# A Fourier mix and a gated block with W_out multiplied by seven products for eight: a second level of the scheme for two of the seven sums, and one PSUM bank per step

## The chip, the cores and the metric

The kernel runs on one core of one Trainium2 chip. The metric is the device time of one execution in microseconds; the time before is the median of three runs. TensorE (PE) multiplies matrices out of SBUF into PSUM[...]. VectorE (DVE) and ScalarE (ACT) can read PSUM; GpSimd (POOL) works on SBUF; SyncE (SP) issues transfers. Each engine works through its own list of instructions in order, and semaphores tie the lists together.

## What is computed

```python
X = np.fft.fft(x, axis=1)          # x: 8 x 3008 x 256, fp32
X = np.fft.fft(X, axis=2)
x = X.real.reshape(24064, 256)
h = x @ w_in                       # 256 x 2048
g = h * (1 / (1 + np.exp(-1.702 * h)))
out = g @ w_out                    # 2048 x 256
```

The transform over the sequence is done first. That over the 256 features is folded into `w_in`. A row k and its mirror row S - k share their cosine part P and their sine part Q: the hidden values are P + Q for one and P - Q (with a term for the Nyquist column, called nb below) for the other. So each step makes P and Q for 256 rows and gets 512 rows of hidden values from them: a forward half and a backward half, which VectorE stores in reversed order.

The products with `w_out` follow the Strassen-Winograd scheme: for a pair of hidden blocks f and the two halves of the rows, the eight 128 x 128 x 256 products become seven, with sums of hidden values (s1 to s4) and of weights (t1 to t4, made once). The seven sums m1 to m7 are kept over eight steps, one group, and added together at the group's end.

## The kernel before: the parts that matter

The loop has 8 x 3 x 2 x 8 = 384 steps (batch, block, half, pair p of hidden blocks). Eight steps make a group. The output products of step t run in loop step t + LAG, LAG = 3. PSUM has four rotating banks (pa, pb, and the transform's) and one bank for each of o0 to o3.

```python
psm = ctx.enter_context(tc.tile_pool(name="psm", bufs=4, space=PS))
pso = ctx.enter_context(tc.tile_pool(name="pso", bufs=1, space=PS))
# [cut]
def halves(out, lhs, rhs, **how):
    for c0 in (0, 64):
        nc.tensor.matmul(out[c0:c0 + 64], lhsT=lhs[:, c0:c0 + 64], rhs=rhs, **how)

def hidden(t):                                     # P into pa, Q into pb
    # [cut]
    for ps, cs in ((pa, 0), (pb, 1)):
        for i in range(2):
            f = 2 * p + i
            halves(ps[:, i * 256:i * 256 + n], wcs[cs][:, f * 128:(f + 1) * 128], pq[:, cs, ks], start=True, stop=True)
    v = sp.tile([128, 512], F32, tag="v", name="v")
    nc.scalar.copy(two(v[:], n), two(pa[:], n))
    vb[t] = v, pa, pb

def rows(t):                                       # forward P + Q, dif = nb * af2 - Q, backward P + dif, reversed
    # [cut]
    nc.vector.tensor_tensor(two(h[:], n), two(v[:], n), two(pb[:], n), op=ALU.add)
    for i in range(2):
        f = 2 * p + i
        nc.vector.scalar_tensor_tensor(dif[:, i * 256:i * 256 + n], nb[:, ks], af2[:, f:f + 1],
                                       pb[:, i * 256:i * 256 + n], op0=ALU.mult, op1=ALU.subtract)
    # [cut: one reversed tensor_tensor of pa and dif into h[:, 1]]

def activate(t):
    # [cut]
    nc.scalar.activation(g, g, ACTF.Gelu_apprx_sigmoid)        # all 1024 columns in one

def sums(t, eng):                                  # s1, s3 on GpSimd; s2, s4 on VectorE
    # [cut]

def product(t):
    # [cut]
    s = st.pop(t)
    plan = ((0, 0, wo[:, p, 0, :], h[:, 0, 0, :n], 0), (0, 1, wt[:, p, 1, :], s[:, 1, :n], 0),
            (1, 0, wo[:, p, 2, :], h[:, 0, 1, :n], 0), (1, 1, wt[:, p, 2, :], s[:, 2, :n], 0),
            (2, 0, wt[:, p, 0, :], s[:, 0, :n], 0), (2, 1, wo[:, p, 3, :], s[:, 3, :n], 0),
            (3, 0, wt[:, p, 3, :], h[:, 1, 1, :n], 0))
    # [cut]
    for q, i, lhs, rhs, f in plan:
        halves(pot[q][:, i, :n], lhs, rhs, start=(p == 0 and i == 0 and f == 0), stop=(p == NP - 1), skip_group_check=True)
    # [cut: at p == NP - 1 ScalarE copies the first sum out of bank o0]

def combine(t):                                    # at the group's end: seven additions and two transposes
    # [cut]
    for out_, i0, i1, how in ((u2, c1, m6, ALU.add), (c11, c1, m2, ALU.add), (u3, u2, m7, ALU.add),
                              (u2, u2, m5, ALU.add), (c12, u2, m3, ALU.add), (c22, u3, m5, ALU.add),
                              (c21, u3, m4, ALU.subtract)):
        nc.vector.tensor_tensor(out_, i0, i1, op=how)
    # [cut]

for t in range(n + LAG):
    if t < n:
        hidden(t)
    # [cut]
    if t >= LAG:
        product(t - LAG)
    # [cut]
    if 0 < t <= n:
        activate(t - 1)
        sums(t - 1, nc.gpsimd)
    sums(t - 2, nc.vector)
    if t < n:
        rows(t)
    if t >= LAG:
        combine(t - LAG)
    for fn, args in extra.get(t, ()):              # transform of the next block or batch: fold1, mix1, stage2, ...
        fn(*args)
```

Of the kernel before, what the change touches and what calls it, by code (L numbers as in the profile page):

```python
# [27 lines left out]
F32 = mybir.dt.float32  # L28
# [15 lines left out]
LAG = 3  # L44
# [67 lines left out]
def kernel(ctx: ExitStack, tc, x, w_in, w_out, tab1, tab2, out):  # L112
# [13 lines left out]
    sp = ctx.enter_context(tc.tile_pool(name="sp", bufs=2, space=SB))  # L126
    op = ctx.enter_context(tc.tile_pool(name="op", bufs=2, space=SB))
    cv = ctx.enter_context(tc.tile_pool(name="cv", bufs=1, space=SB))
    psm = ctx.enter_context(tc.tile_pool(name="psm", bufs=4, space=PS))
    pso = ctx.enter_context(tc.tile_pool(name="pso", bufs=1, space=PS))  # L130
    ctx.enter_context(tc.manual_schedule())

    Xr = [nc.dram_tensor(f"Xr{b}", (NA, NJ, D), F32, kind="Internal").ap() for b in range(B)]
# [16 lines left out]

        return w[rows, jj * NM:jj * NM + 64]

    def bank(name):
        return psm.tile([128, 512], F32, tag="mm", name=name)

# [275 lines left out]
    def differences(n):  # L433
        ps = slice(2 * n, 2 * n + 2)
        b11, b12, b21, b22 = (wo[:, ps, q, :] for q in range(4))
        t1, t2, t3, t4 = (wt[:, ps, q, :] for q in range(4))
        for out, i0, i1 in ((t1, b12, b11), (t2, b22, t1), (t3, b22, b12), (t4, t2, b21)):
            nc.gpsimd.tensor_tensor(out, i0, i1, op=ALU.subtract)

    def fold_w(n):  # L440
# [16 lines left out]

    NP = NF // 2
    steps = [(b, blk, hh, p) for b in range(B) for blk in range(NBLK) for hh in range(2) for p in range(NP)]
    vb, ht, st, pot, ot = {}, {}, {}, {}, {}  # L460

    def width(blk, hh):

        return 225 if (blk, hh) == (0, 1) else 256

    def two(ap, n):
        return free(ap, 0, [256, 2], [1, n])

    def halves(out, lhs, rhs, **how):
        for c0 in (0, 64):  # L470
            nc.tensor.matmul(out[c0:c0 + 64], lhsT=lhs[:, c0:c0 + 64], rhs=rhs, **how)  # L471

    def hidden(t):

        b, blk, hh, p = steps[t]
        n = width(blk, hh)
        pq, ks = pqt[b, blk], slice(hh * 256, hh * 256 + n)
        pa, pb = bank("pa"), bank("pb")
        for ps, cs in ((pa, 0), (pb, 1)):
            for i in range(2):  # L480
                f = 2 * p + i
                halves(ps[:, i * 256:i * 256 + n], wcs[cs][:, f * 128:(f + 1) * 128], pq[:, cs, ks], start=True, stop=True)
        v = sp.tile([128, 512], F32, tag="v", name="v")

        nc.scalar.copy(two(v[:], n), two(pa[:], n))  # L485
        vb[t] = v, pa, pb

    def rows(t):
        b, blk, hh, p = steps[t]
        n = width(blk, hh)  # L490
        nb, ks = nbt[b, blk], slice(hh * 256, hh * 256 + n)
        v, pa, pb = vb.pop(t)
        h = ht[t] = hp.tile([128, 2, 2, 256], F32, tag="h", name="h")
        dif = sp.tile([128, 512], F32, tag="dif", name="dif")
        nc.vector.tensor_tensor(two(h[:], n), two(v[:], n), two(pb[:], n), op=ALU.add)  # L495
        for i in range(2):
            f = 2 * p + i
            nc.vector.scalar_tensor_tensor(dif[:, i * 256:i * 256 + n], nb[:, ks], af2[:, f:f + 1],  # L498
                                           pb[:, i * 256:i * 256 + n], op0=ALU.mult, op1=ALU.subtract)

        full, rest = divmod(n, RUN)
        for at, blocks, m in ((0, full, RUN), (full * RUN, 1, rest)):
            if m:
                ins = [free(x[:], at, [256, 2], [RUN, blocks], [1, m]) for x in (pa, dif)]
                nc.vector.tensor_tensor(free(h[:], 512 + at + m - 1, [256, 2], [RUN, blocks], [-1, m]), *ins, op=ALU.add)  # L505

    def activate(t):
        b, blk, hh, p = steps[t]
        g = free(ht[t][:], 0, [256, 4], [1, width(blk, hh)])
        nc.scalar.activation(g, g, ACTF.Gelu_apprx_sigmoid)  # L510

    def sums(t, eng):

        if not NP <= t < len(steps):
            return
        h, n = ht[t], width(*steps[t][1:3])
        a11, a12, a21, a22 = h[:, 0, 0, :n], h[:, 0, 1, :n], h[:, 1, 0, :n], h[:, 1, 1, :n]
        if eng is nc.gpsimd:
            st[t] = sp.tile([128, 4, 256], F32, tag="s", bufs=3, name="s")
        s1, s2, s3, s4 = (st[t][:, q, :n] for q in range(4))  # L520
        if eng is nc.gpsimd:
            eng.tensor_tensor(s1, a21, a22, op=ALU.add)  # L522
# [2 lines left out]
            eng.tensor_tensor(s2, s1, a11, op=ALU.subtract)  # L525
            eng.tensor_tensor(s4, a12, s2, op=ALU.subtract)  # L526

    def product(t):

        b, blk, hh, p = steps[t]  # L530
        n = width(blk, hh)
        if p == 0:
            for q in range(4):
                pot[q] = pso.tile([128, 2, 256], F32, tag=f"o{q}", name=f"po{q}")
        h = ht.pop(t)
        if t < NP:

            plan = [(half, dh, wo[:, p, 2 * f + dh, :], h[:, half, f, :n], f)
                    for half in range(2) for dh in range(2) for f in range(2)]
        else:  # L540
            s = st.pop(t)
            plan = ((0, 0, wo[:, p, 0, :], h[:, 0, 0, :n], 0), (0, 1, wt[:, p, 1, :], s[:, 1, :n], 0),
                    (1, 0, wo[:, p, 2, :], h[:, 0, 1, :n], 0), (1, 1, wt[:, p, 2, :], s[:, 2, :n], 0),
                    (2, 0, wt[:, p, 0, :], s[:, 0, :n], 0), (2, 1, wo[:, p, 3, :], s[:, 3, :n], 0),
                    (3, 0, wt[:, p, 3, :], h[:, 1, 1, :n], 0))

        if t == len(steps) - 2:
            pot["plan"] = plan
            return
        if t == len(steps) - 1:  # L550
            plan = [it for two_ in zip(pot.pop("plan"), plan) for it in two_]

        for q, i, lhs, rhs, f in plan:
            halves(pot[q][:, i, :n], lhs, rhs, start=(p == 0 and i == 0 and f == 0), stop=(p == NP - 1), skip_group_check=True)
        if p < NP - 1 or t < NP:
            return
        c1 = pot["c"] = op.tile([128, 256], F32, tag="u0", bufs=1, name="u0")
        nc.scalar.copy(c1[:, :n], pot[0][:, 0, :n])  # L558

    def combine(t):  # L560

        b, blk, hh, p = steps[t]
        if p < NP - 1:
            return
        n = width(blk, hh)
        o = op.tile([128, 4, 256], F32, tag="os", name="os")

        def turned(half, src):

            nc.vector.transpose(free(o[:], half * 512, [32, 2], [64, 8], [1, 32]), free(src, 0, [256, 2], [32, 8], [1, 32]))  # L570
            store(b, blk, hh, o, half)

        if t < NP:
            for half in range(2):
                turned(half, pot[half][:])
            return
        c = cv.tile([128, 4, 256], F32, tag="m", bufs=2, name="c")
        if n < 256:
            nc.gpsimd.memset(c[:, :, n:], 0.0)
        (_, m6), (m2, m7), (m5, m3), (m4, _) = ((pot[q][:, 0, :n], pot[q][:, 1, :n]) for q in range(4))  # L580
        u2, u3 = (op.tile([128, 256], F32, tag=f"u{q}", bufs=1, name=f"u{q}")[:, :n] for q in (1, 2))
        c1 = pot["c"][:, :n]
        c11, c12, c21, c22 = (c[:, q, :n] for q in range(4))
        for out_, i0, i1, how in ((u2, c1, m6, ALU.add), (c11, c1, m2, ALU.add), (u3, u2, m7, ALU.add),
                                  (u2, u2, m5, ALU.add), (c12, u2, m3, ALU.add), (c22, u3, m5, ALU.add),
                                  (c21, u3, m4, ALU.subtract)):
            nc.vector.tensor_tensor(out_, i0, i1, op=how)  # L587
            if t == len(steps) - 1:
                if out_ is c12:
                    turned(0, c[:])  # L590
                elif out_ is c22 or out_ is c21:
                    i = int(out_ is c22)
                    nc.vector.transpose(free(o[:], 512 + 32 * i, [64, 8], [1, 32]), free(c[:], (2 + i) * 256, [32, 8], [1, 32]))
        if t == len(steps) - 1:
            store(b, blk, hh, o, 1)
            return
        for half in range(2):
            turned(half, c[:, 2 * half:])

    def store(b, blk, hh, o, half):  # L600

# [136 lines left out]
    at(4, rotate, 0, 4, NG)  # L738
    for i in range(NCK):
        at(7 + i, differences, i)  # L740
    for b in range(B):
        t0 = b * NBLK * NF
        late = 0 if b else 3
# [12 lines left out]
        for blk in range(NBLK):  # L756
            nxt = (b, blk + 1) if blk + 1 < NBLK else (b + 1, 0)
            if nxt[0] < B:
                at(t0 + blk * NF + 8, stage2, *nxt)
                at(t0 + blk * NF + 12, nyquist, *nxt)  # L760

    for t in range(n + LAG):
        if t < n:
            hidden(t)
        if t == 0:
            low_up(in2)
            nyquist(0, 0)
            low_down(in2)
        if t in rows_at:
            first_row(rows_at[t])  # L770
        if t >= LAG:
            product(t - LAG)
        if t in early:
            fold_w(early[t])

        if 0 < t <= n:
            activate(t - 1)
            sums(t - 1, nc.gpsimd)
        sums(t - 2, nc.vector)
        if t < n:  # L780
            rows(t)
        if t >= LAG:
            combine(t - LAG)
        for fn, args in extra.get(t, ()):
            fn(*args)

# [27 lines left out]
```

## Time and profile before

| | before |
|---|---|
| time, median of 3 runs | 1921.33 us (1920.55 to 1921.42) |
| span of the profiled execution | 1919.2 us, granted TensorE clock 0.998 |
| VectorE | 1409.3 us (73%), 2937 instructions |
| GpSimd | 768.2 us (40%), 1057 instructions |
| ScalarE | 674.7 us (35%), 932 instructions |
| output products, 256 columns (L471, tile po) | 8992 records of 379 ns |
| weight loads of 64 columns | 137 ns each |
| gelu of 1024 columns (L510) | 320 of 1060 ns |
| sums on GpSimd, 256 columns (L522, L523) | 624 of 733 and 750 ns |
| sums on VectorE, 256 columns (L525, L526) | 624 of 456 and 487 ns |

The page of the profile gives busy times per engine, a picture of the span in 40 slices, the chain of work that ended last, and the costliest groups of instructions by line, engine and shape. Records of TensorE overlap: a record lasts longer than the time from one to the next, so prices of products are read from starts, not from lengths. An fp32 product appears as two records, and each product is issued in two halves of 64 weight columns. A group's row ends with the idle time of its engine just ahead of it and the instruction that ended that wait.

### The profile page before, as it was taken

Reading aid. Unit: us, or ns where it says so; the run is one execution under the profiler, and the core shown is the slowest. Engines: PE = TensorE matmul, PEld = TensorE weight load, DVE = VectorE, ACT = ScalarE, POOL = GpSimd, SP = SyncE. Lnnn points to the kernel's source line nnn. Section 1 sums busy time; section 2 is a strip of 40 time slices with the busy share of each in tenths; the row PEclk is TensorE's granted clock in tenths of the full one; section 3 lists DMA queues with packets and bytes.
Section 4 is the critical chain, followed back from the end, with each engine's and each line's share of the span. In section 5 each row is a group of like instructions: output and inputs, shape, how many; then the busy total and the mean of one; then the engine's idle time right before and its main releaser. Section 6 shows DMA issues by size and latency. Waiting matters only on the chain.

```text
span 1919.2 us, 46708 instructions
## 1 busy us (share of the span) xinstructions
PE 1907.5 (99%) x19184; PEld 1284.4 (67%) x19184; DVE 1409.3 (73%) x2937; ACT 674.7 (35%) x932; POOL 768.2 (40%) x1057
## 2 busy tenths in 40 slices
PE   9999999999999999999999999999999999999998
PEld 6676666766666666666667666676666766667665
DVE  7777777776787677767777677677777777778766
ACT  6533333333333333333333333333333333333332
POOL 4474324632256223552235523264323642223222
PEclk9999999999999999999999999999999999999999
DMA  8621630345212542126222272122820223202201
GB/s 282 163 52 37 115 34 12 60 62 99 18 22 51 99 61 25 48 33 103 41 29 50 44 107 33 16 51 44 126 18 13 18 53 53 18 13 28 18 12 23
DMA packets 145380, 104.66 MB, mean 55 GB/s; under 512 B 104914, under 2 KB 127986, under 8 KB 143984
## 3 DMA queue, kind: packets, MB, share of 16 engines
q1 hardware_dynamic: 143952, 101.14, 31.2%
q8 instruction: 153, 2.51, 0.6%
q10 hardware_dynamic: 1216, 0.52, 0.1%
q14 instruction: 59, 0.48, 0.1%
HBM read 58.38 MB, written 48.01 MB: 55 GB/s over the span
## 4 chain that ended last, share of the span: by engine, by line
PE 98%; DMA 1%; ACT 0%; DVE 0%; issue 0%; SPq 0%; ACTq 0%
PE po L471 59%; PE pa L471 17%; PE pb L471 17%; PE ps L226 2%; PE ps L328 1%; PE ps L279 1%; PE warm L297 1%; DMA raw<-in_moe_w_out_dram 0%; PE psw L444 0%; DMA t<-Td 0%; PE psr L314 0%; PE psf L454 0%; DMA Td<-e 0%; ACT h L510 0%; ACT r L384 0%
## 5 line engine op out<-in xcount | busy, mean ns | idle before, releaser
L471 PE MATMUL po<-s,wo 128*64 128x256 f32 (+1 forms) x6016 | 763.6, 375 | 0.0
L522 POOL TENSOR_TENSOR s<-h 128x256 f32<-128x256 f32 (+1 forms) x376 | 271.4, 722 | 1080.9 <-ACT h L510 1021.2
L471 PE MATMUL po<-h,wo 128*64 128x256 f32 (+1 forms) x4768 | 697.1, 375 | 0.0
L485 ACT COPY v<-pa 128x512 f32<-128x512 f32 (+1 forms) x384 | 222.1, 578 | 1061.3 <-PE pa L471 1061.3
L471 PEld LDWEIGHTS po<-s,wo 128*64 128x64 f32 x6016 | 433.0, 137 | 203.0
L495 DVE TENSOR_TENSOR h<-v,pb 128x512 f32<-128x512 f32 (+1 forms) x384 | 258.9, 674 | 405.3 <-PE pb L471 393.7
L471 PEld LDWEIGHTS po<-h,wo 128*64 128x64 f32 x4768 | 343.0, 137 | 161.2
L510 ACT ACTIVATE h<-h 128x1024 f32<-128x1024 f32 (+1 forms) x384 | 401.1, 1045 | 19.3 <-DVE h L505 17.0
L471 PE MATMUL pa<-pq,wcs 128*64 128x256 f32 (+1 forms) x3072 | 393.5, 377 | 1.9 <-ACT h L510 1.7
L471 PE MATMUL pb<-pq,wcs 128*64 128x256 f32 (+1 forms) x3072 | 390.3, 375 | 0.0
L498 DVE SCALAR_TENSOR_TENSOR dif<-nb,af,pb 128x256 f32<-128x256 f32 (+1 forms) x768 | 328.1, 468 | 0.9 <-ACT nb L346 0.9
L471 PEld LDWEIGHTS pa<-pq,wcs 128*64 128x64 f32 x3072 | 215.5, 137 | 115.9 <-issue 16.1
L471 PEld LDWEIGHTS pb<-pq,wcs 128*64 128x64 f32 x3072 | 221.2, 137 | 103.7 <-ACT xt L229 0.2
L523 POOL TENSOR_TENSOR s<-h 128x256 f32<-128x256 f32 (+1 forms) x376 | 277.1, 737 | 0.0
L505 DVE TENSOR_TENSOR h<-pa,dif 128x512 f32<-128x512 f32 (+1 forms) x448 | 265.4, 604 | 13.2
L526 DVE TENSOR_TENSOR s<-h,s 128x256 f32<-128x256 f32 (+1 forms) x376 | 192.0, 511 | 12.9
L525 DVE TENSOR_TENSOR s<-s,h 128x256 f32<-128x256 f32 (+1 forms) x376 | 180.8, 481 | 4.3 <-POOL s L522 4.3
L199 POOL TENSOR_TENSOR xt<-xt 111x510 f32<-111x510 f32 x56 | 74.6, 1332 | 4.4
L587 DVE TENSOR_TENSOR c<-u,po 128x256 f32<-128x256 f32 (+1 forms) x188 | 69.4, 409 | 2.5 <-PE po L471 0.9
L334 DVE STREAM_TRANSPOSE pq<-ps 128x256 f32<-128x256 f32 x96 | 34.6, 417 | 46.9 <-PE ps L328 46.9
L587 DVE TENSOR_TENSOR u<-u,po 128x256 f32<-128x256 f32 (+1 forms) x141 | 57.6, 409 | 8.3 <-ACT u L558 2.5
L570 DVE STREAM_TRANSPOSE os<-c 128x512 f32<-128x512 f32 x93 | 60.3, 686 | 0.0
(73 smaller groups left out, 516.0 us busy)
## 6 DMA issues: line engine op xcount, KB each, us to landing
out_dram<-os SPq DMA_DIRECT2D x284, 64.0 KB
Td<-xt SPq DMA_DIRECT2D x14, 768.0 KB
t<-Td SPq DMA_DIRECT2D x7, 1536.0 KB
xt<-in_x_dram SPq DMA_DIRECT2D x14, 512.0 KB
xt<-Xr SPq DMA_DIRECT2D x14, 512.0 KB
nb<-pq SPq DMA_DIRECT2D x23, 256.0 KB
out_dram<-os SPq DMA_DIRECT2D x96, 56.0 KB
Xr<-in_x_dram SPq DMA_DIRECT2D x7, 752.0 KB
```

What stands on the lines that cost most here:

```text
L199: eng.tensor_tensor(low, low, free(t, up + D - 1, [-D, 2], [-1, D - 1]), op=ALU.add)
L471: nc.tensor.matmul(out[c0:c0 + 64], lhsT=lhs[:, c0:c0 + 64], rhs=rhs, **how)
L485: nc.scalar.copy(two(v[:], n), two(pa[:], n))
L495: nc.vector.tensor_tensor(two(h[:], n), two(v[:], n), two(pb[:], n), op=ALU.add)
L498: nc.vector.scalar_tensor_tensor(dif[:, i * 256:i * 256 + n], nb[:, ks], af2[:, f:f + 1], pb[:, i * 256:i * 256 + n], op0=ALU.mult, op1=AL ...
L505: nc.vector.tensor_tensor(free(h[:], 512 + at + m - 1, [256, 2], [RUN, blocks], [-1, m]), *ins, op=ALU.add)
L510: nc.scalar.activation(g, g, ACTF.Gelu_apprx_sigmoid)
L522: eng.tensor_tensor(s1, a21, a22, op=ALU.add)
L523: eng.tensor_tensor(s3, a11, a21, op=ALU.subtract)
L525: eng.tensor_tensor(s2, s1, a11, op=ALU.subtract)
L526: eng.tensor_tensor(s4, a12, s2, op=ALU.subtract)
L587: nc.vector.tensor_tensor(out_, i0, i1, op=how)
```

## The change

**The second level.** Two of the seven products of a step, those with a12 (into m2) and with a22 (into m4), use operands that need no sums of the first level. In 46 of the 48 groups (`deep`) they are taken over two steps together, and the scheme is used once more: 64-column blocks of weights and 128-row blocks of hidden values. For m2 and m4 side by side, each pair of steps has seven products of half the width and half the rows in the place of eight. They need sums of hidden values (`deeper`, on VectorE), of weights (`small_weights`, on GpSimd, once), two more banks o3 and o4 in place of parts of the old ones, and a combination of their own at the group's end (`combine_small`), which also exchanges partition halves by three copies on ScalarE. `combine_last` adds the outcome in the steps after that.

**One bank per step.** P is written into one bank (b0 or b1 in turn) by `begin`, a step ahead. VectorE makes g = 2P + nb * af2 out of it (`doubled`), then `second` adds Q onto P in the same bank. ScalarE takes gelu(P + Q) straight from PSUM (`forward`) and VectorE stores g - (P + Q) reversed (`backward`), with a gelu of its own a step later (`activate_back`). The term nb * af2 is now made by ScalarE two steps ahead (`middle`). The copy of P, the addition of P and Q and the two `dif` operations are gone.

**Orders.** The output products come in two parts around `begin`, the first additions at the group's end take two outputs at once, and the narrow half block has 226 columns for 225.

Its aim is fewer TensorE cycles per step, and the banks for it.

```diff
-    psm = ctx.enter_context(tc.tile_pool(name="psm", bufs=4, space=PS))
-    pso = ctx.enter_context(tc.tile_pool(name="pso", bufs=1, space=PS))
+    psp = ctx.enter_context(tc.tile_pool(name="psp", bufs=1, space=PS))
 [cut]
+    def begin(t):
+        n = width(t)
+        x = xb[t] = bank("x", f"b{t % 2}")
+        for i in range(2):
+            halves(x[:, i * 256:i * 256 + n], *operands(t, 0, i), start=(i == 0), stop=False)
+    def second(t):
+        n = width(t)
+        for i in range(2):
+            halves(xb[t][:, i * 256:i * 256 + n], *operands(t, 1, i), start=False, stop=True)
+    def middle(t):
 [cut]
+            nc.scalar.activation(g[:, i * 256:i * 256 + n], nbt[b, blk][:, hh * 256:hh * 256 + n], ACTF.Copy,
+                                 scale=af2[:, f:f + 1])
+    def doubled(t):
 [cut]
+        nc.vector.scalar_tensor_tensor(g, two(xb[t][:], n), 2.0, g, op0=ALU.mult, op1=ALU.add)
+    def forward(t):
 [cut]
+        nc.scalar.activation(two(h[:], n), two(xb[t][:], n), ACTF.Gelu_apprx_sigmoid)
+    def backward(t):
+        reversed_sum(t, gt.pop(t), xb.pop(t), ALU.subtract)
+    def activate_back(t):
+        g = free(ht[t][:], 512, [256, 2], [1, width(t)])
+        nc.scalar.activation(g, g, ACTF.Gelu_apprx_sigmoid)
 [cut]
+    def deeper(t, part):
 [cut: s3, s1 in part 0, s2, s4 in part 1, each of 2 x 128 columns]
+            nc.vector.tensor_tensor(out, i0, i1, op=how)
 [cut]
+    def small_products(t, ks):
 [cut]
+                nc.tensor.matmul(sub(k)[64 * side:64 * side + 64, :w], lhsT=lhs, rhs=rhs,
+                                 start=(p == 0 and k in (1, 2)), stop=(p == NP - 2), skip_group_check=True)
 [cut]
+            plan = [(0, 0, wo[:, p, 0, :], h[:, 0, 0, :n]), (1, 0, wt[:, p, 2, :], s[:, 2, :n]),
+                    (0, 1, wt[:, p, 1, :], s[:, 1, :n]), (1, 1, wt[:, p, 0, :], s[:, 0, :n]),
+                    (2, 0, wo[:, p, 3, :], s[:, 3, :n])]
 [cut]
     def combine(t):
 [cut]
+        nc.scalar.copy(c1, pot[0][:, 0:n])
+        m5 = free(pot[1][:], 256, [0, 2], [1, n])
+        plan = [(u2, c1, m[6], ALU.add), (u3, u2, m[7], ALU.add),
+                (free(c[:], 256, [512, 2], [1, n]), u[:, 1:3, :n], m5, ALU.add),
+                (c[:, 1, :n], c[:, 1, :n], m[3], ALU.add)]
 [cut]
+    def combine_small(t):
 [cut]
+        nc.scalar.copy(e, sub(1)[:, :w])
+        d22 = d[:, 256 + w:256 + 2 * w]
+        for out, i0, i1 in ((two_of(d, 0, 512), two_of(d, 896, 0), two_of(pot[3], 0, 128)),
+                            (two_of(d, 640, 128), two_of(d, 512, 0), two_of(pot[3], 256, 128)),
+                            (two_of(d, 256, w - 256), two_of(d, 640, 128), two_of(pot[4], 0, 128)),
+                            (d22, d[:, 768:768 + w], sub(5)[:, :w])):
+            nc.vector.tensor_tensor(out, i0, i1, op=ALU.add)
+        nc.scalar.copy(saved[64:128, :n], d[0:64, 256:256 + n])
+        nc.scalar.copy(d[0:64, 256:256 + n], d[64:128, 0:n])
+        nc.scalar.copy(d[64:128, 0:n], saved[64:128, :n])
 [cut]
+        else:
+            if t < n:
+                if t + 2 < n:
+                    middle(t + 2)
+                second(t)
+            product(t - LAG, 0)
+            if t + 1 < n:
+                begin(t + 1)
+            product(t - LAG, 1)
+            small_products(t - LAG, (1, 2, 4, 7))
+            small_products(t - LAG - 1, (5, 6, 3))
 [cut]
+            if t < n:
+                forward(t)
+            if NP < t <= n:
+                activate_back(t - 1)
+                sums(t - 1, nc.gpsimd)
+            if t < n:
+                backward(t)
+        if NP <= t + 1 < n:
+            doubled(t + 1)
+        if t >= NP:
+            sums(t - 2, nc.vector)
+            deeper(t - 2, 0)
+            deeper(t - 3, 1)
         if t >= LAG:
             combine(t - LAG)
+            combine_small(t - LAG - 1)
+            combine_last(t - LAG - 2, 0)
+            combine_last(t - LAG - 3, 1)
```

## The prediction, made before any run

> **What bounds the kernel now.** I read the page's busy times first, then its chain of work that ended last, then the longest pieces of that chain.
>
> ```profile
> PE 1907.5 (99%) x19184; PEld 1284.4 (67%) x19184; DVE 1409.3 (73%) x2937; ACT 674.7 (35%) x932; POOL 768.2 (40%) x1057
> ...
> PE 98%; DMA 1%; ACT 0%; DVE 0%; issue 0%; SPq 0%; ACTq 0%
> ...
> 140.72 3.02 PE po L471 x28
> 145.47 3.02 PE po L471 x28
> 156.14 3.02 PE po L471 x28
> 160.89 3.02 PE po L471 x28
> ```
>
> TensorE has work all the time and the chain is 98% TensorE. The products of one step start 4.75 us after those of the step before (145.47 - 140.72, 160.89 - 156.14). There are 384 steps, so 1824 of the 1919 us are a row of steps without a gap. Only fewer TensorE cycles can help, and any wait that reaches TensorE is paid in full.
>
> Next the timeline around one step, for the price of a product and of a hand-over (start, length, engine):
>
> ```profile
> 1001.66 1.22 PEld L471 LDWEIGHTS po<-s,wo 128*64 128x64 f32 x12
> 1001.87 1.47 PE L471 MATMUL po<-s,wo 128*64 128x256 f32 x12
> 1003.17 0.60 PE L471 MATMUL po<-h,wo 128*64 128x256 f32 x4
> 1003.60 1.03 PE L471 MATMUL pa<-pq,wcs 128*64 128x256 f32 x8
> 1004.74 0.59 ACT L485 COPY v<-pa 128x512 f32<-128x512 f32 x1 [2.69 <-PE pa L471]
> ```
>
> A product of 128x128 weights with 256 columns is two halves of two records each. Twelve records take 1.47 us, four 0.60, so a record costs 0.87/8 = 0.108 us and a product 0.43. A step has four products for P and Q and seven for the output: 11 x 0.431 = 4.74, the step seen above. A record lasts 0.38 us where a pair of halves follows every 0.216, so 0.17 us of drain stand behind the last one; ScalarE begins 0.11 us after the modelled end (1004.63 to 1004.74): 0.28 us from the last issue slot to a reader.
>
> Last the groups by form, for the small operations, and VectorE's timeline where a group of eight steps ends:
>
> ```profile
> L498 DVE SCALAR_TENSOR_TENSOR dif<-nb,af,pb 128x256 f32<-128x256 f32 x640 | 276.8, 473 | 0.9 <-ACT nb L346 0.9
> L505 DVE TENSOR_TENSOR h<-pa,dif 128x512 f32<-128x512 f32 x320 | 221.1, 691 | 11.0
> L587 DVE TENSOR_TENSOR c<-u,po 128x256 f32<-128x256 f32 x156 | 58.4, 414 | 2.2 <-PE po L471 0.9
> L558 ACT COPY u<-po 128x256 f32<-128x256 f32 x39 | 14.5, 372 | 45.2 <-PE po L471 45.2
> ...
> 1032.62 0.94 DVE L587 TENSOR_TENSOR u<-u,po 128x256 f32<-128x256 f32 x2
> 1033.59 1.08 DVE L587 TENSOR_TENSOR c<-u,po 128x256 f32<-128x256 f32 x3
> ```
>
> An addition of 256 columns lasts 0.41 us. Independent ones follow every 0.33 (three in 1.08); dependent ones, end to start plus 0.04, every 0.45.
>
> [...] Here the stretch 32.6 to 36.0 ran at 0.50, after one with some 1 us of matmuls.
>
> **The change, part by part.** 46 of the 48 groups (368 steps) get the second level.
>
> *TensorE, removed and added.* Per step the products with a12 and a22 (2 x 0.431) give way to seven small pairs per two steps: 64-column halves against 128 rows. Four records of 127 or 129 columns with full 128-column loads start every 0.447 us in the opening (13.13, 13.58, 14.02, 14.47), 0.112 each; half of 0.216 is 0.108. I take 0.22 for a small pair: 3.5 x 0.22 = 0.77. A step becomes 9 x 0.431 + 0.77 = 4.65, 0.09 less. Times 304 full-width steps: -27 us. The 64 narrow steps go from 225 to 226 columns and to 113-row products[...]: about 0. At the very best (exact halves) 0.108 x 368 = -40.
>
> *VectorE and ScalarE, in sum.* VectorE loses the 259 us additions and the 328 us `dif`, gains doublings (estimate 0.74 us[...]: 278), second-level sums (736 x 0.43 = 316) and 1.3 us per group of combining (60): about 1490 us. ScalarE loses 222 of copies, gains about 370 of middle terms, 77 for two gelus instead of one, 70 of combining: about 970. Neither is a bound by sum. Order decides.
>
> *The order at a group's end.* Each engine works its list in order. Call A, B, C, D the loop's steps with t mod 8 = 2, 3, 4, 5: in A the old group's last large products are done and `combine` is issued, in B its last small ones and `combine_small`. An ordinary step is safe: Q ends at 0.86 + 0.28, gelu to 1.74, reversal to 2.52; the next P ends at 2.59 + 0.28, doubling to 3.61; the next Q wants it at 4.65.
>
> First wait, in B. In A VectorE reaches 3.61, then two sums (0.456 and 0.487 on average) to 4.5, two second-level sums to 5.35, u2 to 5.76, u3 to 6.2, the double sum of 512 that reads bank o1 to 6.9. o0 to o2 exist once; B's second product writes o1 and is due at 4.76 + 0.86 + 0.43 = 6.05. Wait: about 0.95 us. In 14 groups a `mix1` of over 1 us lies between and hides it. 32 x 0.95 = 30 us.
>
> Second wait, in D. From the end of B all is serial, because ScalarE's list has the copies of `combine_small` ahead of C's middle terms and gelu: drain 0.28; copy e of 128 columns 0.27; hand-over 0.08; four additions 1.5; 0.09; three dependent copies between partition halves 3 x 0.44 = 1.32[...]; two middle terms[...] 0.72; C's gelu of 512 0.60; 0.09; C's reversal 0.61 (0.69 less overlap); doubling for D 0.74; 0.10 to TensorE. Sum 6.40. TensorE has only step C to do meanwhile, 9 x 0.431 + 4 x 0.22 = 4.76. It waits 1.65 us for D's Q, 46 times: 76 us.
>
> *Elsewhere.* Sixteen more `small_weights` operations on GpSimd in steps 9 to 12, where it already folds, delay first sums: +5. In fold stretches a VectorE sum of two SBUF operands stretches (1.42 us at 1038.48, beside a GpSimd addition of 1.27), and there are twice as many: +5.
>
> Sum: 1921 - 27 + 30 + 76 + 10 = 2010 us.
>
> **Rivals.** (1) *The waits vanish*: scattered copies and additions run faster, or TensorE finds other work.[...] Against: 6.40 would have to fall under 4.76, and with each operation at its least I still get about 5.9. Time then: o1 wait gone, 46 x 1.1 = 51, net 1945 to 1950; with no wait at all 1885 to 1895. (2) *The clock falls*:[...] I think it seldom happens. If it did each time: +1.7 x 46 = 78, 2090. (3) *Small products are bound by weight loads*: 137 ns instead of 108 per record makes a small pair 0.27, a step 4.84, +0.1 x 368 = +37 instead of -27: 2070. Against it: the records of 127 to 129 columns in the opening start every 0.112 with loads of 192 ns. (4) *VectorE falls behind in every fold stretch*: 56 steps by a further us, about 2060.
>
> **Range and chances.** The sign rests on one serial list whose members each have a row: the waits come to 50 (all small) to 150 us (each operation a tenth longer, and the first wait in all groups), against a gain of at most 40. Range 1965 to 2065. Faster by over 2% needs no waits at all: 0.02. Within 2% (up to 1960): 0.09. Slower: 0.89.
>
> **What would show it.** TensorE busy falls and the chain has ScalarE and VectorE in it; waits of TensorE for the doubling of VectorE, about 46 of 1.5 to 2 us, once in 38 us, and some 30 of about 1 us for the additions that read o1; ScalarE idle before `saved`, waiting for VectorE; starts of small pairs 0.22 apart; ordinary steps 4.65 apart. I am wrong if the copies of `combine_small` do not hold up the gelu of C, if steps are not 4.65 apart outside the group's end, or if the clock is below 1.0.

## The result, and the profile after

| | before | after |
|---|---|---|
| time, median of 4 runs each | 1920.94 us (1919.94 to 1921.42) | 2066.69 us (2062.82 to 2070.01) |
| ratio | | 1.0759, 95% interval 1.0734 to 1.0783 |
| span of the profiled execution | 1919.2 us | 2067.7 us |
| mean granted TensorE clock | 0.998 | 0.986 |

The change makes the kernel slower by 7.6%. The prediction had said slower, through two waits at the end of each group, but by 89 us (range 1965 to 2065 us); it is 146, and the time lies 1.7 us above the range.

First the page of the kernel after: busy times, then the chain of work that ended last.

```profile
PE 1928.9 (93%) x21392; PEld 1399.4 (68%) x21392; DVE 1548.5 (75%) x3011; ACT 875.3 (42%) x1868; POOL 796.1 (38%) x1073
...
PE 70%; DVE 17%; ACT 7%; issue 2%; DMA 1%; POOL 1%; SPq 1%; DVEq 0%; ACTq 0%; POOLq 0%
```

TensorE was 99% busy and 98% of the chain. Now it is 93% busy, and a quarter of the chain is VectorE and ScalarE: they have become, in places, what TensorE waits for. VectorE's 1548.5 us are no bound by sum. The waits of TensorE by releaser (us in total, times, longest) say where:

```profile
PE x L478 <- DVE g L548: 82.3, 52, 3.0
PE po L478 <- DVE c L703: 25.3, 40, 0.7
```

The first is the wait of step D for the doubling, the second that of step B for bank o1. There is nothing of the kind in the kernel before. The view counts from the modelled end of the last product, some 0.17 us after its last issue slot (a record of 0.38 us, a pair of them every 0.216), so each wait costs TensorE 0.17 more than it shows. Below, waits are counted from start to start, less what the columns take at the granted clock.

Now TensorE's timeline through steps C and D of one undisturbed group (start, length, engine, line, tile, count, and in brackets the idle time and its releaser):

```profile
1956.14 0.64 PE L623 MATMUL po<-h,wo 128*64 128x128 f32 x8
1956.58 0.42 PE L623 MATMUL po<-h,held 128*64 128x128 f32 x4
1956.80 0.42 PE L623 MATMUL po<-r,held 128*64 128x128 f32 x4
1958.52 1.08 PE L478 MATMUL x<-pq,wcs 128*64 128x256 f32 x8 [1.31 <-DVE g L548]
```

Eight records of small products take 0.44 us, four 0.22: the small pair costs what was predicted. Then nothing is left to do until VectorE has doubled P. The chain that ends in that product shows why (start, length, piece):

```profile
1952.79 0.43 DVE held L727
...
1953.77 0.63 DVE held L727 x2
...
1954.48 0.41 ACT held L728
...
1954.91 0.41 ACT held L729
...
1955.76 0.91 ACT g L542 x2
1956.67 0.49 ACT h L555
...
1957.18 0.69 DVE h L503
1957.87 0.61 DVE g L548
...
1958.52 1.08 PE x L478 x8
```

This is the predicted serial list, member by member: four additions, the three partition-half copies (the third ends with the 1955.76), two middle terms, C's gelu, its reversal, the doubling. From the first addition to the product it takes 5.73 us; the prediction's members for the same stretch add up to 5.77.

The wait of this group is 1.48 us from start to start, and so it is in most groups. In batches 1 to 6 two groups, whose step D is step 13 or 21 of the batch, wait 3.2 us. They end in a fold stretch: a fold is a row of GpSimd additions that prepares a later batch, and `mix1` is the transform's products behind it, whose two results ScalarE copies out of PSUM. VectorE's and then GpSimd's timeline of one at step 21:

```profile
914.47 2.36 DVE L595 TENSOR_TENSOR r<-h 128x256 f32<-128x256 f32 x2
916.75 1.48 DVE L727 TENSOR_TENSOR held<-held,po 128x226 f32<-128x226 f32 x4
920.95 0.69 DVE L503 TENSOR_TENSOR h<-g,x 128x512 f32<-128x512 f32 x1 [2.72 <-ACT h L555]
```

```profile
914.24 1.44 POOL L203 TENSOR_TENSOR xt<-xt 111x510 f32<-111x510 f32 x1
...
916.50 0.91 POOL L206 TENSOR_TENSOR xt<-xt 111x254 f32<-111x254 f32 x1
```

The two second-level sums `r` take 2.36 us; in the undisturbed group at 1951.94 they take 0.75. They begin after GpSimd's fold addition of 1.44 us has begun and end at 916.8, in its row of additions; taken singly, they end at 915.96 and 916.82, each about 0.28 us after a GpSimd addition has ended. The additions of `combine_small` stand behind them in VectorE's list, so the serial chain begins some 1.6 us late, and the view shows 3.00 us of idle time and not 1.31:

```profile
922.29 1.97 PE L478 MATMUL x<-pq,wcs 128*64 128x256 f32 x8 [3.00 <-DVE g L548]
```

The `r` sums, with both inputs in SBUF, stretch by 1.6 us beside the fold; the additions of `combine_small` that follow, with one input in PSUM, begin at 916.75, beside the fold addition that runs from 916.50 to 917.41, and take their usual time (1.48 us for four, as in the other groups of 226 columns). That the sums wait for GpSimd's additions is read from these times; how they hold each other up was not shown.

Behind most of these waits the clock was down. The windows of the trace, 3.41 us each, give the busy time of TensorE first; the clock is the first number after POOL's:

```profile
918.02:921.43 3.41, 1.27 (x20) 0.89 (x16) 0.69 (x3) 3.04 (x8) 0.00 (x0) 1.00 0.00 0
921.43:924.84 3.41, 2.55 (x12) 1.46 (x14) 3.31 (x8) 1.33 (x5) 1.64 (x2) 0.50 0.00 0
...
1423.19:1426.60 3.41, 1.48 (x22) 1.03 (x18) 0.69 (x3) 2.83 (x7) 0.00 (x0) 1.00 0.00 0
1426.60:1430.01 3.41, 2.35 (x22) 1.63 (x24) 3.34 (x7) 2.22 (x6) 1.66 (x3) 1.00 0.00 0
```

TensorE was busy for 1.27 of 3.41 us, and the next window ran at half clock. With 1.48 of 3.41 (second pair) it did not. Nine of the twelve waits of 3.2 us have half clock behind them. With one at the start there are ten such stretches before the end of the run, 54.6 us together.

The whole difference, term by term, from TensorE's starts and the clock record. The last column is of the experiment without folds, further down, against the kernel before:

| us | predicted | after | after, without folds |
|---|---|---|---|
| TensorE's own work | -27 | -26 | -26 |
| wait in B (o1) | +30 | +40 | +37 |
| wait in D (doubling) | +76 | +87 | +75 |
| other waits (start, fold stretches) | +10 | +25 | +9 |
| half clock (half of TensorE's work in those stretches) | 0 | +22 | +3 |
| sum | +89 | +148 | +98 |
| difference of the two spans | | +148.5 | +97.2 |

### The profile page after: what moved, and what is told of

It reads as the page before. It is cut to its first block, busy times and chain, and to the rows that moved or that the text cites. A ratio compares the mean times of both kernels' runs of the same rounds, so it can differ in the third digit from the quotient of the medians.

```text
span 2067.7 us, 51061 instructions
## 1 busy us (share of the span) xinstructions
PE 1928.9 (93%) x21392; PEld 1399.4 (68%) x21392; DVE 1548.5 (75%) x3011; ACT 875.3 (42%) x1868; POOL 796.1 (38%) x1073
## 4 chain that ended last, share of the span: by engine, by line
PE 70%; DVE 17%; ACT 7%; issue 2%; DMA 1%; POOL 1%; SPq 1%; DVEq 0%; ACTq 0%; POOLq 0%
PE po L478 31%; PE x L478 26%; PE po L623 10%; DVE r L595 3%; DVE held L727 3%; DVE g L548 3%; ACT g L542 2%; DVE h L503 2%; ACT h L555 1%; DVE c L703 1%; PE ps L230 1%; PE ps L332 1%; DVE s L577 1%; DVE u L703 1%; ACT held L729 1%
## 5 line engine op out<-in xcount | busy, mean ns | idle before, releaser
L478 PE MATMUL x<-pq,wcs 128*64 128x256 f32 (+1 forms) x6016 | 789.1, 382 | 84.5 <-DVE g L548 82.3
L478 PEld LDWEIGHTS x<-pq,wcs 128*64 128x64 f32 x6016 | 433.6, 139 | 260.5 <-DVE g L548 94.5
L555 ACT ACTIVATE h<-x 128x512 f32<-128x512 f32 (+1 forms) x376 | 220.2, 586 | 749.9 <-PE x L478 729.8
L503 DVE TENSOR_TENSOR h<-g,x 128x512 f32<-128x512 f32 (+2 forms) x440 | 254.5, 590 | 330.2 <-ACT h L555 329.5
L542 ACT ACTIVATE g<-nb,af 128x256 f32<-128x256 f32 (+1 forms) x752 | 335.1, 495 | 1.4 <-DVE h L512 0.8
L548 DVE SCALAR_TENSOR_TENSOR g<-x,g 128x512 f32<-128x512 f32 (+1 forms) x376 | 254.4, 677 | 95.0 <-PE x L478 94.7
L478 PE MATMUL po<-h,wo 128*64 128x256 f32 (+1 forms) x1824 | 267.6, 382 | 2.5 <-DVE u L703 2.2
L562 ACT ACTIVATE h<-h 128x512 f32<-128x512 f32 (+1 forms) x376 | 230.9, 614 | 0.2 <-DVE h L503 0.2
L595 DVE TENSOR_TENSOR r<-h 128x256 f32<-128x256 f32 (+1 forms) x368 | 195.8, 573 | 0.0
L478 PEld LDWEIGHTS po<-h,wo 128*64 128x64 f32 x1824 | 134.5, 138 | 71.7 <-DVE u L703 17.8
```

What stands on the lines that cost most here:

```text
L542: nc.scalar.activation(g[:, i * 256:i * 256 + n], nbt[b, blk][:, hh * 256:hh * 256 + n], ACTF.Copy, scale=af2[:, f:f + 1])
L548: nc.vector.scalar_tensor_tensor(g, two(xb[t][:], n), 2.0, g, op0=ALU.mult, op1=ALU.add)
L555: nc.scalar.activation(two(h[:], n), two(xb[t][:], n), ACTF.Gelu_apprx_sigmoid)
L595: nc.vector.tensor_tensor(out, i0, i1, op=how)
```

## The experiments

All are compared with the kernel before, run beside them on the same chip (median 1920.6 to 1920.8 us throughout). Each has at least four runs of its own.

### One wait at a time

*Later copies.* The three partition-half copies go out of `combine_small` and are issued a step later, behind the gelus of C in ScalarE's list. Nothing is left out.

```diff
+        def exchange(t):            # the three copies of combine_small, alone
 [cut]
                 activate_back(t - 1)
                 sums(t - 1, nc.gpsimd)
+            exchange(t - LAG - 2)
             if t < n:
                 backward(t)
```

> The three partition-half copies of combine_small are issued one step later on ScalarE, behind that step's gelus, and nothing else is moved. Theory (ScalarE's list holds the gelu of step C, and TensorE waits for the doubling behind it): the 46 waits in D (87 us in all in the profile of the changed kernel) go, and the stretches at half clock (about 22 us) with them: 1960 to 1985 us, clock 0.998. Rival (VectorE is simply behind in the stretches where GpSimd folds, and the copies are only where it shows): the wait comes back at another place, 2020 us or more.

Measured: 1977.74 us, ratio 1.0298 (1.0283 to 1.0314), clock 0.996. The waits of TensorE:

```profile
PE po L478 <- DVE c L703: 25.4, 40, 0.7
PE x L478 <- DVE g L548: 7.1, 19, 0.8
```

Counted start to start, D's wait falls from 87 to 6 us, B's stays at 40, the cost of the clock falls from 24 to 8. So 1.3 us of copies at the wrong place in ScalarE's list were worth 89 us of the kernel's time.

*Early additions.* `combine` is issued ahead of VectorE's sums of the step, so the banks o0 to o2 come free sooner. Copies as in the change.

```diff
+        if t >= LAG:
+            combine(t - LAG)
         if t >= NP:
             sums(t - 2, nc.vector)
 [cut]
         if t >= LAG:
-            combine(t - LAG)
             combine_small(t - LAG - 1)
```

> combine is issued ahead of the two levels of sums in VectorE's list, nothing else is moved. Theory (B waits for bank o1 because the sums stand ahead of combine's additions): the waits in B (40 us) go, D's wait stays or grows a little since the sums now come later: 2020 to 2040 us. Rival (the additions are late because VectorE has too much to do in A, whatever the order): 2060 us or more.

Measured: 2030.59 us, ratio 1.0569 (1.0553 to 1.0585), clock 0.989. B's wait is gone (0.8 us), and D's is 95:

```profile
PE x L478 <- DVE g L548: 90.9, 54, 3.0
```

40 us of waits went, 8 came back in D, where TensorE now arrives earlier at the same chain, and the time fell by 36.

*Both.*

> Both moves. Theory: both waits go and so do the clock's falls; what is left against the kernel before is the gain of TensorE, 26 us, less what remains of waits in the fold stretches: 1915 to 1945 us. Rival (VectorE as a bound in the fold stretches): 1960 us or more.

Measured: 1934.08 us, ratio 1.0068 (1.0053 to 1.0083), clock 0.997. The two edits alone win 89 and 36, together 133. Of the two group-end waits about 6 us are left, nearly all in D; with the rest, 133 of the 146 us are gone. They are orders in two lists; nothing of the computation differs.

### The second level left out

`deep` returns False: seven products per step again, with one bank per step and the new orders kept.

```diff
     def deep(t):
-        return NP <= t < last
+        return False
```

> The second level is left out: all seven products of a step are taken at the first level, with one bank per step and the new orders kept. The result is the same computation. Theory: no combine_small, so no wait in D and no fall of the clock; the work of TensorE is that of the kernel before, and the wait in B may remain because its additions are still behind sums: 1925 to 1965 us. Rival (the bank per step with Q waiting for the doubling costs by itself): 1970 us or more, with waits for the doubling in every step.

Measured: 1957.39 us, ratio 1.0193 (1.0176 to 1.0210), clock 0.998. In step D nothing waits for the doubling (1.1 us in all), since there is no `combine_small`; 20 us remain in step B and the step behind it, and at step 16 the run is already some 12 us behind the kernel before; that is most of its 37 us. One bank per step thus makes no wait in each step. As a price of the second level the run says little, because its waits differ too.

### Are the folds what the sum lacked?

*After, seven of eight fold pieces of each later batch left out.* GpSimd is then idle where it was busiest. This kernel leaves work out: seven eighths of the additions that prepare batches 1 to 7.

```diff
             for c in range(NCH):
-                at(t0 + 7 + 2 * c + late, fold1, b + 1, c, nc.gpsimd)
+                if c == 0:
+                    at(t0 + 7 + late, fold1, b + 1, c, nc.gpsimd)
```

> Seven of the eight fold pieces of each later batch are left out of the changed kernel, so GpSimd is idle where it was busiest; the output is then not the reference's, all else is unchanged. Theory (the excess over my sum is made in the fold stretches, where VectorE's sums wait for GpSimd, and by the clock falls that follow there): only the undisturbed waits stay, 0.86 us in step B and 1.48 us in step D of all 46 groups, 108 us, less the 26 us that TensorE saves: 1990 to 2005 us, clock 0.995 or more, and no wait of 3 us for the doubling. Rival (the two waits alone, whatever GpSimd does): above 2045 us, with the waits of 3 us still in two groups per batch.

*Before, with the same pieces left out*, as a control.

> The same seven of eight fold pieces left out of the kernel before, as a control: the folds lie beside TensorE's work there, so 1915 to 1921 us. If the folds cost time in themselves, it falls by 20 us or more, and the run above proves less.

Measured: after without folds 2022.38 us, ratio 1.0526 (1.0508 to 1.0543), span 2016.4, clock 0.997; before without folds 1920.84 us, ratio 0.9999 (0.9991 to 1.0008). Leaving them out gains nothing in the kernel before and 44 us in the one after (51 by the two profiled spans). The waits of after without folds:

```profile
PE x L478 <- DVE g L548: 67.8, 47, 2.5
PE po L478 <- DVE c L703: 23.2, 34, 0.7
```

The time is above the expected range, which had taken 1.48 us for each wait in D. Group by group, the waits at step 21 fall from 3.15 us to 1.72, but those at step 13 only from 3.2 to 2.5, and three stretches at half clock remain. ScalarE's and VectorE's timelines ahead of one of the latter show a second cause:

```profile
1086.07 1.08 ACT L233 COPY xt<-ps 128x512 f32<-128x512 f32 x2 [2.86 <-PE ps L230]
```

```profile
1088.36 0.69 DVE L503 TENSOR_TENSOR h<-g,x 128x448 f32<-128x448 f32 x2 [1.49 <-ACT h L555]
```

The two copies of `mix1`, issued in step A, stand ahead of step B's middle terms and gelu in ScalarE's list. VectorE waits 1.49 us for that gelu, and `combine_small` comes later by it. The steps 8 to 15 of a batch are also narrow ones (226 columns), so TensorE has less to do meanwhile: in the last batch, which has neither folds nor `mix1`, the wait at step 13 is still 1.9 us. The same `mix1` hides the wait in B (none at step 11, 0.1 us at step 19, against 1.04 elsewhere).

The second-level sums in the answer by tile, after and then after without folds (shortest, median and longest in ns):

```profile
L595 DVE TENSOR_TENSOR r<-h x368: 380/418/2157, 112.6 to 2021.8; 128x256 f32<-128x256 f32 x152, 128x226 f32<-128x226 f32 x32
```

```profile
L595 DVE TENSOR_TENSOR r<-h x368: 381/418/943, 111.1 to 1970.5; 128x256 f32<-128x256 f32 x152, 128x226 f32<-128x226 f32 x32
```

The median is the same, the longest falls from 2157 to 943 ns: a median hides the whole effect.

### Can the rest be won back?

*Start.* On top of both order edits the first group stays at one level, and the weights of the second level are made at steps 13, 15, 17 and 19.

```diff
-        return NP <= t < last
+        return 2 * NP <= t < last
 [cut]
-        at(9 + i, small_weights, i)
+        at(13 + 2 * i, small_weights, i)
```

> Later copies and early additions together (1934 us), and the first group of full steps stays at one level while the weights of the second level are made at steps 13, 15, 17, 19 and not at 9 to 12. Theory (what is left over the kernel before is partly the start, where GpSimd makes these weights and folds at once, with a wait of 5.0 us and a clock fall behind it): 1918 to 1925 us, no wait above 2 us at 110 to 130 us, no clock fall there. Rival (the start is late for another cause): 1930 us or more.

Measured: 1925.38 us, ratio 1.0021 (1.0014 to 1.0028), clock 0.998, 0.4 us above the expected range. In the version with both order edits, TensorE's timeline had shown at the start

```profile
116.95 0.60 PE L478 MATMUL po<-s,wo 128*64 128x226 f32 x4 [1.56 <-POOL s L575]
...
125.72 0.69 PE L230 MATMUL ps<-xt,w 47*64 47x256 f32 x3 [4.88 <-POOL xt L206]
```

with half clock from 124.6 to 131.4. Both waits and this stretch are gone.

*Start and folds elsewhere.* The fold pieces of later batches move away from the steps that evacuate banks.

```diff
             for c in range(NCH):
-                at(t0 + 7 + 2 * c + late, fold1, b + 1, c, nc.gpsimd)
+                at(t0 + (0, 6, 8, 14, 16, 22, 24, 30)[c] if b else 10 + 2 * c, fold1, b + 1, c, nc.gpsimd)
                 if c % 2:
-                    at(t0 + 8 + 2 * c + late, mix1, b + 1, c // 2)
-            at(t0 + 24 + late, spill, b + 1)
-            at(t0 + 29 + late, fill, b + 1)
+                    at(t0 + (10, 18, 26, 32)[c // 2] if b else 11 + 2 * c, mix1, b + 1, c // 2)
+            at(t0 + 33 if b else 27, spill, b + 1)
+            at(t0 + 36 if b else 32, fill, b + 1)
             if b + 2 < B:
-                at(t0 + 33 + late, load_x, b + 2)
-            at(t0 + 36 + late, rotate, b + 1)
+                at(t0 + 37 if b else 36, load_x, b + 2)
+            at(t0 + 39, rotate, b + 1)
```

> As the one above, and the fold pieces of each later batch are moved to steps 0, 6, 8, 14, 16, 22, 24 and 30 of a batch, away from the steps in which VectorE and ScalarE evacuate the banks; spill, fill and rotation follow at 33, 36 and 39. Theory (the rest of the loss is 3.5 us of waits per batch in the fold stretches): 1895 to 1910 us, below the kernel before. Rivals: the fold waits only move (1915 to 1925 us), or the shorter way from spill to the next batch's second stage makes a new wait once per batch (1925 us or more, seen ahead of the second-stage products).

Measured: 1906.82 us, ratio 0.9928 (0.9913 to 0.9943), clock 0.999. This beats the kernel before by 14 us, under 1% but clear of the noise. Its page:

```profile
PE 1879.5 (99%) x21344; PEld 1405.3 (74%) x21344; DVE 1525.2 (80%) x2992; ACT 876.5 (46%) x1864; POOL 799.6 (42%) x1073
...
PE 92%; DVE 5%; DMA 1%; ACT 1%; POOL 0%; issue 0%; SPq 0%; DVEq 0%; POOLq 0%; ACTq 0%
```

TensorE is 99% busy again, with 28 us of busy time less than before (1907.5).

*The change as it was, with start and folds moved only*, and *the kernel before with its folds moved in the same way*:

> The changed kernel with nothing altered but the start (first group at one level, weights of the second level later) and the fold pieces, moved away from the steps that evacuate the banks; copies and additions stay in the order of the change. Theory (the two waits of each group are as I summed them, and the excess is made where folds meet the evacuation): waits of 0.8 to 0.9 us in B and about 1.5 us in D in all groups, no wait of 3 us, clock 0.99 or more: 2005 to 2025 us. Rival (the folds cost as much wherever they lie): 2045 us or more.

> The kernel before with the fold pieces moved in the same way, as a control: its TensorE hardly waits, so 1917 to 1925 us. If it gains as much as the changed one (10 us or more), the gain is one of the fold schedule alone and not of the second level.

Measured: 2023.97 us, ratio 1.0546 (1.0526 to 1.0565), clock 0.994, against 1921.52 us, ratio 1.0003 (0.9995 to 1.0012). With all folds done but elsewhere, the changed kernel is as fast as with seven eighths of them left out (2022), so for the most part it is their place that costs, not their amount. The new start is in this run too. It won 9 us on top of both order edits; if it is worth as much here, which no run shows, the move alone wins 34 of the 43 us. D's waits are then about 1.5 us in each group without a `mix1` in its step A and 1.8 to 3.0 in those with one (steps 13, 21 and 29), where 1.5 was expected, 78.9 in all; the clock falls at five of those of step 13. B's are 26 us. The `mix1` pieces moved with the folds, and both of their effects moved along: B's wait is now hidden at step 27 too, and D's is 2.0 us at step 29, where it was 1.48. The kernel before gains nothing from the move.

### The clock by itself

Three products of 256 columns, whose results nothing uses, are put into the spare bank b2 in step D, ahead of the products that wait.

```diff
 [cut: warm_more(n), n products of 256 columns into bank "b2"]
                 if t + 2 < n:
                     middle(t + 2)
+                if NP < t < last and t % 8 == 5:
+                    warm_more(3)
                 second(t)
```

> The changed kernel with three products of 256 columns more in step D of each group, into the spare bank b2, ahead of the products that wait for the doubling; their results are used by nothing. About 1.3 us of work in a wait of 1.5 us or more. Theory (the ten stretches at half clock follow the long waits of step D and cost 20 to 24 us in themselves): the stretches go, clock 0.995 or more, and the time falls to 2035 to 2055 us. Rival 1 (the clock's falls cost little, as they lie in waits): 2060 to 2070 us. Rival 2 (the products delay what follows them in the groups with short waits): 2070 us or more.

Measured: 2100.22 us, ratio 1.0933 (1.0914 to 1.0951), clock 0.986. The expectation missed, and the run does not answer its question: in one group of six batches the spare bank is held by the rotation's result, for which the filler waited 4.4 us (26.4 in all, released by VectorE's copy into `t`), and the clock fell behind each of these waits. The falls of the fold stretches were gone. Without that group (`and t % 48 != 37`):

> As the run with three more products in step D, but without them in the one group of a batch in which the spare bank is still held by the rotation (there they had waited 4.4 us, six times, and the clock fell behind each). Theory (the clock's falls cost 20 to 24 us of the changed kernel, and come from the waits of step D): no stretch at half clock but one or two at the start, and 2040 to 2055 us. Rival (the falls cost nothing of their own): 2060 us or more although the clock stays up.

Measured: 2054.23 us, ratio 1.0694 (1.0678 to 1.0710), clock 0.998. The only stretch at half clock ahead of the end is one at the start (122.8 to 129.7). The fillers' own work is 38 groups x 3 x 0.43 = 49 us, and waits shrink by 45.5 (178.0 to 132.5). So 3.5 us were added and still 14.9 us of span were won: the clock's falls cost about 18 us on their own (16 by the medians, which are 12.5 us apart), where half of TensorE's work in those stretches gives 20 (24, less the 4 of the start that stay).

### Does the second level bring the gain?

The best version without the second level:

> The best version so far (1907 us: later copies, early additions, start and moved folds) without the second level: all seven output sums at one level, one bank per step and the new orders kept. Theory (bank, orders and fold places are neutral once nothing waits, and the second level brings some 20 us): 1918 to 1930 us. Rival (the gain over the kernel before is one of orders and fold places, not of the second level): 1900 to 1912 us.

Measured: 1970.38 us, ratio 1.0260 (1.0242 to 1.0277). Neither theory: the run has a wait of its own. Without a second level `combine` holds the group's two transposes too, and issued early they stand ahead of the sums `s`:

```profile
PE po L478 <- DVE s L577: 37.2, 28, 2.2
```

With the transposes two and three steps later, as the best version has them:

```diff
             nc.vector.tensor_tensor(out, i0, i1, op=ALU.add)
-            turned(t, o, i, c[:, 2 * i:])
+            if t >= last:
+                turned(t, o, i, c[:, 2 * i:])
 [cut: combine_last turns them for these groups too]
```

> As the best version without its second level, but with the two transposes of a group two and three steps later, as the best version has them, and not ahead of VectorE's sums s, where they had made TensorE wait 1.5 us for s in 28 groups (42 us). Theory (bank, orders and fold places are neutral once nothing waits, and the second level brings the gain): 1920 to 1935 us. Rival (orders and fold places bring the gain, or a good part of it): 1912 us or less.

Measured: 1930.11 us, ratio 1.0052 (1.0035 to 1.0069), clock 0.999. This run and the best version (1906.82) differ by the second level alone, in 45 groups: it brings 23 us. Orders, banks and fold places without it are 9 us slower than the kernel before. Some 5 to 6 of them are there by step 24 of the 384, so most of this loss is one of the start; its cause stays open.

## Why the prediction was right, and where it was wrong

The direction and both group-end waits came as predicted, by the predicted mechanism. What failed is the price of the fold stretches (+5 in the sum), and with it the judgement that the clock would seldom fall (0 in the sum, +22 measured).

*TensorE's work, -27.* Right: -26. The small pair costs 0.22 us, steps that no group end touches start 4.54 and 4.76 us apart in turn (mean 4.65), and the second level alone brings 23 us in 45 groups.

*The wait in D, 1.65 x 46 = 76.* The mechanism is right: the list's length was right to 0.04 us over the part that the chain shows, and moving its three copies takes the wait away. Not every member had a row in a trace: the copies (3 x 0.44 us), the two middle terms (0.72) and the doubling (0.74) were estimates of mine; in the group above the copies start 0.43 and 0.44 us apart, the two middle terms last 0.91 together and the doubling 0.68. The size of an undisturbed wait was 1.48 us (1.24 at step 37 of six batches, where a product of the rotation fills a part of it; 1.3 at step 21 of the first and last batch), not 1.65. The total is still 87 us and not 76, because twelve groups wait 3.2 us.

*The wait in B, 32 x 0.95 = 30.* Mechanism and count are right: 34 groups wait, mostly 1.04 us, and `mix1` hides it at step 11 as I had supposed. At step 19 it hides it in half (0.52 us left in six groups; 0.1 without folds). With two longer ones at the start, 40 us. What I missed is that the `mix1` that hides this wait lengthens the next: its copies hold up ScalarE, and `combine_small` behind it (D's wait at step 13 is 2.5 us even without folds, and 1.9 in the last batch, without `mix1`).

*"In fold stretches ... there are twice as many: +5".* This step failed. I had seen a sum stretch to 1.42 us and added up the stretched sums; I did not ask what stood behind them in VectorE's list. There stood `combine_small`, the head of the serial chain that TensorE waits for in D. At step 21 these 1.6 us make most of the difference between a wait of 1.7 us and one of 3.2. Leaving the folds out shows their cost in the waits: about 4 us in B, 12 in D, 16 elsewhere (start included).

*Rival 2, "I think it seldom happens".* This was an estimate: all that the trace of before showed was the one stretch of half clock at 32.6, ahead of the end. For the undisturbed groups it holds (no fall behind a wait of 1.48 us). But the clock fell ten times, nine of them at the twelve waits of 3.2 us and once behind one of 5.0 at the start, 22 us more than before; the prediction's own sign of being wrong, a clock below 1.0, came with 0.986. The two failed steps hang together: the folds make a wait of 1.7 us (step 21) or 2.5 (step 13) one of 3.2. Of the waits of 2.5 three still had half clock behind them without folds, of those of 1.7 none. With the 19 us of clock that go with the folds, they cost 51 us of span; the sum lacked 59. Rival 4 (VectorE behind in every fold stretch, 2060) named the place, and came near the time by a wrong way: by a microsecond in each of 56 steps, where it was 3 us in twelve groups and the clock behind them.

*Rival 1* fell: the waits don't vanish by themselves. They do by order, and then the change is a gain. *Rival 3* fell: a small pair takes 0.22 us, not 0.27. Weight loads don't bound the narrow ones either: two halves of 113 columns start every 0.097 us (eight records in 0.39 from 913.75 on), where a load of 64 columns lasts 137 ns.

The upper end of the range allowed for 150 us of waits. There were 152 more than before, so it about held for the waits, and the clock's 22 us, for which it had no term, went past it.

Some sums of the prediction are off without bearing on this. 384 steps of 4.75 us count the 64 narrow steps too high (they start about 4.2 us apart), so the row is some 1790 us and not 1824. VectorE's terms add up to about 1477 us and not 1490, and 1548.5 were measured; ScalarE took 875.3 and not 970 (335.1 of it the middle terms, for which I had estimated 370). A doubling of full width took 0.69 us (at 912.70), not 0.74. And the stretch ahead of 32.6, read as some 1 us of matmuls, has TensorE busy for 2.58 of 3.40 us in the view by windows.

## What to carry to other kernels

When work is taken from an engine that bounds the kernel, list what each other engine has in its queue ahead of the next thing that the bound engine needs; three copies of 0.4 us ahead of a gelu cost 89 us here that went when they were issued one step later. Price an operation that another engine may hold up by what stands behind it in its list, not by its own stretch. Then look for the order in which the change pays, before judging the idea: the same second level was 7.6% slower as ordered and 0.7% faster with its copies later, its additions earlier, the start changed and the folds elsewhere.

## What was not expected of the hardware

Half clock came also behind windows in which TensorE was busy for up to 0.42 of the time. In after it begins on a grid of 3.413 us (the 208.22 us from the fall at 672.26 to that at 880.48 are 61 steps of it). Laid over this grid, the ten falls ahead of the end came after windows with a busy share of 0 to 0.42, nine of them with 0.15 or more. The emptiest windows between 50 us and the end without a fall behind them had 0.43 (from 1423.19), 0.48 (from 873.65) and 0.50 (from 1877.17). A wait of 3.0 us of which 2.1 lay in one window (up to 922.29) was enough, and with the folds moved one of 2.32 us (up to 1098.94): the eight records of 226 columns behind it last 1.72 us, where eight of them at 1092.24 last 0.93. In after no wait of 1.48 us was followed by a fall. Nor is the busy share a sharp limit elsewhere: in the kernel before half clock began at 32.6 after the 2.58 of 3.40 us (0.76), while on the same grid a window with 0.51 (from 56.52) has no fall behind it. What exactly the clock goes by stays open.
